# GpSimd makes the sign words of a float64-to-float32 weight conversion, and VectorE folds the shift into the or

## The chip, the cores and the metric

The kernel runs on one core of one Trainium2 chip. The metric is device time in microseconds for one execution. A core has five engines that work side by side, each in its own program order: TensorE (PE, matrix products, with its weight loads shown as PEld), VectorE (DVE), ScalarE (ACT), GpSimd (POOL) and SyncE (SP, which here issues the transfers). An engine waits for another only through semaphores.

## The reference

What is computed is linear attention with a root-mean-square norm, and on its output a feed-forward layer whose activation is a rational function:

```python
kv = np.einsum('bhsd,bhse->bhde', k, v)          # q, k, v: (8, 8, 576, 64) float32
out = np.einsum('bhsd,bhde->bhse', q, kv)
rms = np.sqrt(np.mean(out * out, axis=-1, keepdims=True) + 1e-06)
attn = (out / rms * g_norm).astype(np.float32)
...
h = x @ w_in                                     # x: (4608, 512), w_in: (512, 2048)
P = a[0] + a[1] * h + a[2] * h**2 + a[3] * h**3
Q = 1.0 + np.abs(b[0]) * np.abs(h) + np.abs(b[1]) * h**2
g = P / (Q + 1e-06)
return (g @ w_out).astype(np.float32)            # w_out: (2048, 512)
```

The weights `w_in` and `w_out` come as float64. The kernel sees them as pairs of 32-bit words and makes float32 of them on the chip.

## The kernel before, in words

**Tiles.** The 4608 tokens are nine tiles of 512, and the 2048 hidden columns are sixteen chunks of 128. A step of the main loop, here called a slot, is one pair (tile t, chunk c). There are 144, numbered i from 0; slots 0 to 15 belong to tile 0. In slot i, PE makes `h` of slot i+1 (`gemm1`, L409 for tile 0, L413 to L415 later), some of the attention of the next tile, and the share of slot i-2 in the output (`gemm2`, L470 for tile 0 and four chunks of tile 1, L474 to L476 otherwise). In tile 0 the products run in plain float32: four for `h` and four for the output in a slot, each of which the trace shows as two matrix instructions, so x8 is one slot's worth. Later tiles use split operands and three products for each.

**The activation of a slot** runs on ACT and DVE, in the order of the code:

- `ew_a`: ACT makes d = h squared (L423), q = |b0 h| (L424) and u = -a3 h - a2 (L426). DVE makes q = b1 d + q (L425) and u = u h (L427).
- `ew_b`: `fill(-1)`, then DVE u = (u - a1) h (L433). ACT makes d = 1/(1+q) with a logarithm and an exponential (L434, L435), which need L425.
- `ew_c`: DVE L439 (q and d, so it needs L435), `fill(0)`, L441, `fill(1)`, L447, `fill(2)`.

L427 and L433 read `h` in PSUM and `u` in SBUF. L425, L439, L441 and L447 read two tiles in SBUF each. The buffer of `h` is free for the next product after L433.

**The fills.** `rest[k]` lists other DVE work that is put at these four places in a slot's DVE order: the conversion of weights, the remainders of splits, parts of the attention. Every engine's order is the order of the code (a manual schedule).

**The conversion** of a unit of two chunks (128 by 1024 words) has two stages. `conv_a`: ACT scales the high and the low words (L179; for the first unit DVE, L177). `conv_b`, on DVE: L193 shifts the high word left by three, L198 takes the sign bit of the high word and ors it in, L199 adds the low word. There are 16 units, eight of `w_in` ("wi") and eight of `w_out` ("wo"). The first three are converted in halves: the first one ahead of the loop, the first half of the second too, its second half and the first half of the third in slot 0, and the last half in slot 1. The other 13 are converted whole, one in each of the slots 2 to 14, with L193 at `fill(-1)` and L198 and L199 at `fill(0)`. From tile 1 on the loop has no conversions.

What waits for a conversion: L409 of the chunks of a "wi" unit, and L470 of those of a "wo" unit. A unit of slot 3, say, holds w_out chunks 2 and 3, and PE's output product for slot 2 needs it.

Of the kernel before, what the change touches and what calls it, by code (L numbers as in the profile page):

```python
# [9 lines left out]
I32 = mybir.dt.int32  # L10
# [3 lines left out]
ALU = mybir.AluOpType  # L14
# [9 lines left out]
def linear_attention_then_rational_ffn(  # L24
# [13 lines left out]
    PE, ACT, DVE, POOL = nc.tensor, nc.scalar, nc.vector, nc.gpsimd  # L38
# [31 lines left out]
    na = const.tile([P, 4], F32, name="na")  # L70
    POOL.tensor_scalar(na, ab[:, 0:4], -1.0, None, ALU.mult)
    b1abs = const.tile([P, 1], F32, name="b1abs")
# [67 lines left out]
    units = list(schedule)  # L140
# [3 lines left out]
    def at_slot(step, k):  # L144
        return [u for u in units if schedule[u][step] == k]
# [7 lines left out]
    raws, ups, w32, whl, gparts = {}, {}, {}, {}, {}  # L153

    def fetch_w(u):
        kind, c = u
        k = units.index(u) % NG
        raws[u] = wpool.tile([P, 2 * DM], I64, tag=f"g{k}", name=f"raw_{kind}{c}")
        src = w_in[c:c + 2].rearrange("c p k f -> p c (k f)") if kind == "wi" else \
            w_out[c:c + 2].rearrange("c p f -> p c f")  # L160
        to = raws[u].rearrange("p (c f) -> p c f", c=2)
        for js in ((slice(0, 1), slice(1, 2)) if u in units[:2] else (slice(0, 2),)):
            nc.sync.dma_start(to[:, js], src[:, js])
# [5 lines left out]
    def words(u, part):  # L169
        w = raws[u].bitcast(I32).rearrange("p (f w) -> p f w", w=2)[:, part]  # L170
        return w[:, :, 0], w[:, :, 1]

    both, one, two = slice(0, 2 * DM), slice(0, DM), slice(DM, 2 * DM)
# [7 lines left out]
    def conv_a(u, part=both, engine="S"):  # L181
        low, high = words(u, part)
        scale(engine, f32(high), f32(high), 2.0**-112)
        scale(engine, low, low.bitcast(U32), 2.0**-29)

    def conv_b1(u, part=both):
        kind, c = u
        low, high = words(u, part)
        if u not in ups:
            ups[u] = wpool.tile([P, 2 * DM], F32, tag=f"f{units.index(u)}", name=f"{kind}w{c}")  # L190
            for j in range(2):
                w32[kind, c + j] = ups[u][:, j * DM:(j + 1) * DM]
        DVE.tensor_scalar(ups[u].bitcast(I32)[:, part], high, 3, None, ALU.logical_shift_left)  # L193

    def conv_b2(u, part=both):
        low, high = words(u, part)
        w = ups[u].bitcast(I32)[:, part]
        DVE.scalar_tensor_tensor(w, high, -(1 << 31), w, ALU.bitwise_and, ALU.bitwise_or)  # L198
        DVE.tensor_tensor(w, w, low, ALU.add)  # L199

    def conv_b(u, part=both):
        conv_b1(u, part)
        conv_b2(u, part)

    def gpart(k, j):
        if k not in gparts:
# [3 lines left out]
    def split_w(u):  # L210
        kind, c = u
        i = units.index(u)
        w = ups.pop(u)
        if i == NU - 1:
            last = work.tile([P, 2 * DM], F32, tag="rb", name="w_last", bufs=2)
            DVE.tensor_copy(last, w)
            w = last
        fpart = lambda k, what: wpool.tile([P, 2 * DM], F32R, tag=f"f{k}", name=f"{kind}{what}{c}")
        wh = fpart(i - 1, "h") if i == NU - 1 else gpart((i + 1) // 2, (i + 1) % 2)
        ACT.copy(wh, w)  # L220

        def rest():
            wl = gpart(0, 0) if i == 0 else fpart(i if i == NU - 1 else i - 1, "l")
            for j in range(2):
                js = slice(j * DM, (j + 1) * DM)
                whl[kind, c + j] = wh[:, js], wl[:, js]
            DVE.tensor_tensor(wl, w, f32(wh), ALU.subtract)  # L227
        return rest
# [171 lines left out]
    def gemm1(t, c):  # L400
        ph = ps_h.tile([P, TW], F32, tag="h", name=f"h_{t}_{c}")
        gemm1_part(t, c, ph, slice(0, TW))
        return ph
# [14 lines left out]
    def ew_a(t, c, ph, w=TW):  # L418
        nm = f"{t}_{c}"
        d = work.tile([P, w], F32, tag="d", name=f"d_{nm}")  # L420
        q = work.tile([P, w], F32, tag="q", name=f"q_{nm}")
        u = work.tile([P, w], F32, tag="u", name=f"u_{nm}")
        ACT.activation(d, ph, AF.Square)  # L423
        ACT.activation(q, ph, AF.Abs, scale=b0)  # L424
        DVE.scalar_tensor_tensor(q, d, b1abs, q, ALU.mult, ALU.add)  # L425
        ACT.activation(u, ph, AF.Identity, bias=na[:, 2:3], scale=na[:, 3:4])  # L426
        DVE.tensor_tensor(u, u, ph, ALU.mult)  # L427
        pend[t, c] = (d, q, u)

    def ew_b(t, c, ph, fill=lambda k: None):  # L430
        d, q, u = pend[t, c]
        fill(-1)
        DVE.scalar_tensor_tensor(u, u, na[:, 1:2], ph, ALU.add, ALU.mult)  # L433
        ACT.activation(d, q, AF.Ln, bias=bias[:, 2:3], scale=QSC)  # L434
        ACT.activation(d, d, AF.Exp, bias=bias[:, 3:4], scale=-1.0)  # L435

# [13 lines left out]
    def ew_d(t, c, w=TW):  # L450
        u = pend.pop((t, c))[2]
        if (t, c) in gs:
            return
        nm = f"{t}_{c}"
        gh = work.tile([P, w], F32R, tag="gh", name=f"gh_{nm}")
        gl = work.tile([P, w], F32R, tag="gl", name=f"gl_{nm}")
        ACT.copy(gh, u)
        DVE.tensor_tensor(gl, u, f32(gh), ALU.subtract)  # L458
        gs[t, c] = (gh, gl)

    def gemm2(t, c, subs=range(NSUB)):
        g = gs.pop((t, c))
        c = int(c)
        if c == 0:
            acc[t] = [ps_acc.tile([P, DM], F32, tag="acc", name=f"acc_{t}_{s}") for s in range(NSUB)]
        for k, s in enumerate(subs):
            ss = slice(k * P, (k + 1) * P)
            o = acc[t][s]
            if unsplit(t, c):
                PE.matmul(o, g[:, ss], w32["wo", c], start=(c == 0), stop=(c == NF - 1))  # L470
                continue
            gh, gl = g
            wh, wl = whl["wo", c]
            PE.matmul(o, gl[:, ss], wh, start=(c == 0), stop=False)  # L474
            PE.matmul(o, gh[:, ss], wl, start=False, stop=False)  # L475
            PE.matmul(o, gh[:, ss], wh, start=False, stop=(c == NF - 1))  # L476

    def evacuate(t):
        for k in range(NSUB // 2):
            ob = work.tile([P, 2, DM], F32, tag="rb", name=f"ob_{t}_{k}", bufs=2)  # L480
            for s in range(2):
                ACT.copy(ob[:, s], acc[t][2 * k + s])
            r0 = t * TW + 2 * k * P
            nc.sync.dma_start(out[r0:r0 + 2 * P].rearrange("(s p) d -> p s d", s=2), ob)
# [89 lines left out]
    for p in range(NPAIR):  # L574
# [2 lines left out]
        ps = slice(p * Q4, (p + 1) * Q4)  # L577
        PE.matmul(rb, spread[ps], r0[ps], start=True, stop=True)
        DVE.scalar_tensor_tensor(x0[:, p], x0[:, p], ghalf, rb, ALU.mult, ALU.mult)
    conv_b2(units[1], one)  # L580
    conv_a(units[1], two)
    conv_a(units[2])


    slots = [(t, c) for t in range(NTILE) for c in range(NF)]
    ph = gemm1(0, 0)
    for i, (t, c) in enumerate(slots[:-1]):
        ew_a(t, c, ph)
        if i:
            ew_d(*slots[i - 1])  # L590
        rest = {-1: [], 0: [], 1: [], 2: []}
        if i == 0:
            rest[-1].append(lambda: conv_b(units[1], two))
            rest[2].append(lambda: conv_b(units[2], one))
        if i == 1:
            rest[0].append(lambda: conv_b(units[2], two))
        for u in at_slot(2, i):
            rest[-1].append(lambda u=u: conv_b1(u))
            rest[0].append(lambda u=u: conv_b2(u))
        ew_b(t, c, ph, lambda k: [f() for f in rest[k]])  # L600
        for u in at_slot(3, i):
            rest[2].append(split_w(u))
        for u in at_slot(1, i):
            conv_a(u)
        if i >= LAG:
            gemm2(*slots[i - LAG])
            if slots[i - LAG][1] == NF - 1:
                evacuate(slots[i - LAG][0])
        if i < 4:
            ph = gemm1(0, i + 1)  # L610
        if t + 1 < NTILE:
            for step, p in (attention0 if t == 0 else attention)[c]:
                todo_dve = step(t + 1, p)
                if todo_dve:
                    rest[2 if t == 0 else fillat[step]].append(todo_dve)
            for u in at_slot(0, i):
                fetch_w(u)
        if 4 <= i < len(slots) - 2:
            ph = gemm1(*slots[i + 1])
        if c == NF - 2 and t < NTILE - 1:  # L620
            xl = [split(t + 1, p) for p in range(NPAIR)]
            for k in range(2):
                rest[k].append(xl[k])
                rest[2].append(xl[2 + k])
        ew_c(t, c, lambda k: [f() for f in rest[k]])
# [43 lines left out]
```

## Time and profile before

| what | value |
|---|---|
| runs shown | 919.54, 923.49, 924.40 us |
| their median | 923.49 us |
| the profiled execution | 924.01 us |
| its span, first to last instruction | 922.2 us |
| mean granted TensorE clock | 0.989 |
| DVE busy | 799.5 us, 1251 instructions |
| ACT busy | 687.8 us, 1163 instructions |
| POOL busy | 4.5 us, 32 instructions, all of them before the loop |

1.8 us of the profiled execution lie outside the span. Busy time counts an engine's instructions, not its waits. In a timeline row the columns are the start and the length in us, the engine, the line and operation, the tiles out<-in with their size, the number of instructions merged, and in brackets the idle time of that engine before it with what ended it. DVE instructions overlap a little: the next starts before the last has drained, so what a row costs in a chain is the distance from its start to the next start.

### The profile page before, as it was taken

To read this page: it belongs to the slowest core of one execution; us is meant where nothing else is said; L and a number is where in the kernel's file an instruction comes from. 1 tells how busy PE (TensorE), PEld (TensorE's weight loads), DVE (VectorE), ACT (ScalarE), POOL (GpSimd) and SP (SyncE) were. 2 spreads that over 40 slices of the span, in tenths; PEclk is the share of its full clock that TensorE was granted. 3 is DMA by queue.
4 is the path that set the end of the run, shared out by engine and by line. 5 is a ranking of instruction groups with operands and counts; after the bars stand their busy time and mean duration, and the time that the engine had idled before them with its cause. 6 is when DMAs were issued, how large, how long until landed. Compare 5 with 4: busy or idle time off the path is not lost.

```text
span 922.2 us, 11586 instructions
## 1 busy us (share of the span) xinstructions
PE 901.8 (98%) x4268; PEld 677.4 (73%) x4268; DVE 799.5 (87%) x1251; ACT 687.8 (75%) x1163; POOL 4.5 (0%) x32
## 2 busy tenths in 40 slices
PE   6889998999999999999999999999999999999998
PEld 4444444777768788878887888788887888788886
DVE  1798999999988899879977998789888988898887
ACT  2587876888777778777876787777777787777666
POOL 1000000000000000000000000000000000000000
PEclk6999999999999999999999999999999999999999
DMA  8645210320122122211131103220311020101001
GB/s 340 269 161 221 99 35 12 127 69 21 39 86 79 41 47 78 89 41 47 41 126 41 47 30 109 68 48 2 124 53 47 1 69 12 47 0 46 1 1 46
DMA packets 23840, 65.89 MB, mean 71 GB/s; under 512 B 2728, under 2 KB 2728, under 8 KB 23784
## 3 DMA queue, kind: packets, MB, share of 16 engines
q1 hardware_dynamic: 23328, 65.15, 21.5%
q8 instruction: 33, 0.54, 0.2%
q14 instruction: 23, 0.19, 0.1%
q10 hardware_dynamic: 456, 0.00, 0.0%
HBM read 55.58 MB, written 9.57 MB: 71 GB/s over the span
## 4 chain that ended last, share of the span: by engine, by line
PE 83%; DVE 12%; ACT 3%; issue 1%; DMA 1%; DVEq 0%; ACTq 0%
PE h L413 12%; PE h L415 12%; PE h L414 12%; PE acc L474 11%; PE acc L475 11%; PE acc L476 11%; PE acc L470 4%; PE h L409 2%; PE kvp L297 2%; DVE q L425 1%; DVE u L441 1%; DVE q L439 1%; DMA ab<-in_b_dram 1%; PE op L544 1%; DVE u L433 1%
## 5 line engine op out<-in xcount | busy, mean ns | idle before, releaser
L423 ACT ACTIVATE d<-h 128x512 f32<-128x512 f32 x143 | 85.8, 600 | 161.9 <-PE h L415 146.7
L413 PE MATMUL h<-x,parts 128*128 128x512 f32 (+1 forms) x516 | 205.7, 399 | 0.0
L415 PE MATMUL h<-x,parts 128*128 128x512 f32 (+1 forms) x516 | 200.5, 389 | 0.0
L475 PE MATMUL acc<-wol,gh 128*128 128x512 f32 x492 | 191.5, 389 | 0.7 <-DVE wol L227 0.7
L425 DVE SCALAR_TENSOR_TENSOR q<-d,b1abs,q 128x512 f32<-128x512 f32 x143 | 107.2, 750 | 84.8 <-ACT q L424 84.6
L414 PE MATMUL h<-x,wil 128*128 128x512 f32 (+1 forms) x452 | 175.5, 388 | 0.0
L474 PE MATMUL acc<-parts,gl 128*128 128x512 f32 x440 | 171.6, 390 | 0.2 <-DVE gl L458 0.2
L476 PE MATMUL acc<-parts,gh 128*128 128x512 f32 x440 | 171.2, 389 | 0.0
L434 ACT ACTIVATE d<-q,bias 128x512 f32<-128x512 f32 x143 | 105.1, 735 | 30.9 <-DVE q L425 29.4
L413 PEld LDWEIGHTS h<-x,parts 128*128 128x128 f32 x516 | 96.9, 188 | 26.4 <-DVE gl L458 5.0
L426 ACT ACTIVATE u<-h,na 128x512 f32<-128x512 f32 x143 | 112.1, 784 | 0.0
L415 PEld LDWEIGHTS h<-x,parts 128*128 128x128 f32 x516 | 96.9, 188 | 20.6
L475 PEld LDWEIGHTS acc<-wol,gh 128*128 128x128 f32 x492 | 92.4, 188 | 20.0 <-DVE wol L227 1.0
L435 ACT ACTIVATE d<-d,bias 128x512 f32<-128x512 f32 x143 | 103.6, 724 | 4.7
L441 DVE SCALAR_TENSOR_TENSOR u<-u,na,d 128x512 f32<-128x512 f32 x143 | 106.7, 746 | 0.0
L433 DVE SCALAR_TENSOR_TENSOR u<-u,na,h 128x512 f32<-128x512 f32 x143 | 106.1, 742 | 0.2
L439 DVE SCALAR_TENSOR_TENSOR q<-q,d 128x512 f32<-128x512 f32 x143 | 98.6, 689 | 1.1 <-ACT d L435 1.1
L427 DVE TENSOR_TENSOR u<-u,h 128x512 f32<-128x512 f32 x143 | 97.9, 685 | 0.9
L424 ACT ACTIVATE q<-h,ab 128x512 f32<-128x512 f32 x143 | 98.1, 686 | 0.0
L414 PEld LDWEIGHTS h<-x,wil 128*128 128x128 f32 x452 | 85.0, 188 | 16.2 <-issue 0.2
L474 PEld LDWEIGHTS acc<-parts,gl 128*128 128x128 f32 x440 | 82.6, 188 | 18.5 <-DVE gl L458 1.1
L476 PEld LDWEIGHTS acc<-parts,gh 128*128 128x128 f32 x440 | 82.6, 188 | 17.1
(137 smaller groups left out, 1087.4 us busy)
## 6 DMA issues: line engine op xcount, KB each, us to landing
kvm<-in_kv_dram SPq DMA_DIRECT2D x28, 640.0 KB
raw_wo<-in_w_out_dram SPq DMA_DIRECT2D x8, 1024.0 KB
qr<-in_qT_dram SPq DMA_DIRECT2D x32, 256.0 KB
out_dram<-ob SPq DMA_DIRECT2D x16, 512.0 KB
rb<-rd SPq DMA_DIRECT2D x28, 256.0 KB
raw_wi<-in_w_in_dram SPq DMA_DIRECT2D x6, 1024.0 KB
first<-in_first_dram SPq DMA_DIRECT2D x4, 896.0 KB
raw_wi<-in_w_in_dram SPq DMA_DIRECT2D x4, 512.0 KB
```

Of the source, the lines that this page charges most:

```text
L413: PE.matmul(ph, wh, xl, start=(kc == 0), stop=False)
L414: PE.matmul(ph, wl, xh, start=False, stop=False)
L415: PE.matmul(ph, wh, xh, start=False, stop=(kc == NPAIR - 1))
L425: DVE.scalar_tensor_tensor(q, d, b1abs, q, ALU.mult, ALU.add)
L426: ACT.activation(u, ph, AF.Identity, bias=na[:, 2:3], scale=na[:, 3:4])
L433: DVE.scalar_tensor_tensor(u, u, na[:, 1:2], ph, ALU.add, ALU.mult)
L434: ACT.activation(d, q, AF.Ln, bias=bias[:, 2:3], scale=QSC)
L439: DVE.scalar_tensor_tensor(q, q, QEPS, d, ALU.add, ALU.mult)
L441: DVE.scalar_tensor_tensor(u, u, na[:, 0:1], d, ALU.add, ALU.mult)
L474: PE.matmul(o, gl[:, ss], wh, start=(c == 0), stop=False)
L475: PE.matmul(o, gh[:, ss], wl, start=False, stop=False)
L476: PE.matmul(o, gh[:, ss], wh, start=False, stop=(c == NF - 1))
```

## The change

The sign word of a unit, 0 or the sign bit alone, is made by GpSimd from the high word (`high < 0`, times -2^31). DVE then needs two operations instead of three: shift the high word and or the sign word in (one `scalar_tensor_tensor`), and add the low word. For the 13 whole units a manual dependency holds the GpSimd operation until L425 of its slot (`q_made`) is done; those of the first three units wait only for their data. In `ew_b` the DVE operation L433 moves ahead of `fill(-1)`. In slots 2 to 14 the entry at `fill(-1)` calls `conv_b2`, which issues the or there, behind L433, and puts the add (`rest`) at `fill(0)`. So DVE's order in such a slot goes from L425, L427, L193, L433, L439, L198, L199, L441, L447 to L425, L427, L433, or, L439, add, L441, L447. For the halves in slots 0 and 1 `conv_b` issues or and add together at `fill(0)` and `fill(2)`; the second half of the second unit, which stood at `fill(-1)` of slot 0, is now at `fill(0)`.

```diff
@@ conv_b1, conv_b2, conv_b
-        DVE.tensor_scalar(ups[u].bitcast(I32)[:, part], high, 3, None, ALU.logical_shift_left)
+        return POOL.tensor_scalar(ups[u].bitcast(I32)[:, part], high, 0, -float(1 << 31), ALU.is_lt, ALU.mult)
...
-        DVE.scalar_tensor_tensor(w, high, -(1 << 31), w, ALU.bitwise_and, ALU.bitwise_or)
-        DVE.tensor_tensor(w, w, low, ALU.add)
+        DVE.scalar_tensor_tensor(w, high, 3, w, ALU.logical_shift_left, ALU.bitwise_or)
+
+        def rest():
+            DVE.tensor_tensor(w, w, low, ALU.add)
+        return rest
 
     def conv_b(u, part=both):
         conv_b1(u, part)
-        conv_b2(u, part)
+        conv_b2(u, part)()
@@ ew_a
-        DVE.scalar_tensor_tensor(q, d, b1abs, q, ALU.mult, ALU.add)
+        q_made = DVE.scalar_tensor_tensor(q, d, b1abs, q, ALU.mult, ALU.add)
...
+        return q_made
@@ ew_b
         d, q, u = pend[t, c]
+        DVE.scalar_tensor_tensor(u, u, na[:, 1:2], ph, ALU.add, ALU.mult)
         fill(-1)
-        DVE.scalar_tensor_tensor(u, u, na[:, 1:2], ph, ALU.add, ALU.mult)
@@ ahead of the loop, and the loop
-    conv_b2(units[1], one)
+    conv_b2(units[1], one)()
...
+    beside = mybir.DependencyInfo(mybir.DependencyClass.Sync, mybir.DependencyReason.DATA)
...
-        ew_a(t, c, ph)
+        q_made = ew_a(t, c, ph)
+        for u in at_slot(2, i):
+
+            tc.add_manual_dep(conv_b1(u).ins, q_made.ins.name, beside, reason="sign beside h")
...
-            rest[-1].append(lambda: conv_b(units[1], two))
+            rest[0].append(lambda: conv_b(units[1], two))
...
-            rest[-1].append(lambda u=u: conv_b1(u))
-            rest[0].append(lambda u=u: conv_b2(u))
+            rest[-1].append(lambda u=u: rest[0].append(conv_b2(u)))
```

## The prediction

> **What bounds the kernel now.** First the page: which engine is busy, and through which engines the chain that ended last runs.
>
> ```profile
> PE 901.8 (98%) x4268; PEld 677.4 (73%) x4268; DVE 799.5 (87%) x1251; ACT 687.8 (75%) x1163; POOL 4.5 (0%) x32
> ...
> PE 83%; DVE 12%; ACT 3%; issue 1%; DMA 1%; DVEq 0%; ACTq 0%
> ```
>
> PE sets the pace nearly everywhere, so DVE work that goes away is worth only what PE now waits for DVE. The waits of PE from 40 us to the tail give that, all of it:
>
> ```profile
> PE acc L470 <- DVE wow L199: 4.0, 3, 2.5
> PE h L409 <- DVE u L433: 1.7, 1, 1.7
> PE h L414 <- DVE parts L227: 1.2, 1, 1.2
> PE acc L475 <- DVE wol L227: 0.7, 1, 0.7
> PE acc L474 <- DVE gl L458: 0.2, 1, 0.2
> ```
>
> That is 7.8 us, so the largest gain is of that order. About half is the very thing the change speeds up: the output product waits for a converted w_out unit. The longest of the three costs more than its wait:
>
> ```profile
> 60.36 0.80 PE L297 MATMUL kvp<-kvm 128*64 128x64 f32 x20
> 63.64 5.25 PE L470 MATMUL acc<-wow,g 128*128 128x512 f32 x8 [2.48 <-DVE wow L199]
> ```
>
> Windows cut where the granted clock changes show why the eight products behind this gap took 5.25 us (columns: length, then busy time of PE, PEld, DVE, ACT, POOL, then PEclk):
>
> ```profile
> 39.48:42.89 3.41, 2.15 (x5) 1.06 (x6) 3.38 (x6) 1.47 (x3) 0.00 (x0) 1.00 0.01 4
> ...
> 59.96:63.37 3.41, 1.20 (x22) 0.66 (x20) 3.38 (x4) 3.37 (x8) 0.00 (x0) 1.00 0.55 159
> 63.37:66.79 3.42, 3.15 (x4) 1.51 (x5) 3.31 (x8) 1.99 (x4) 0.00 (x0) 0.50 0.31 123
> ```
>
> A stretch with PE 35% busy (1.20 of 3.41) is followed by one at clock 0.50; the stretch with 63% (2.15 of 3.41) kept 1.00. Half speed for 3.42 us loses 1.7 us. The ceiling is so 7.8 + 1.7 = 9.5 us.
>
> **A whole-unit slot, before.** Slot 3 on DVE (start, length):
>
> ```profile
> 57.98 0.75 DVE L425 SCALAR_TENSOR_TENSOR q<-d,b1abs,q 128x512 f32<-128x512 f32 x1
> 58.65 0.68 DVE L427 TENSOR_TENSOR u<-u,h 128x512 f32<-128x512 f32 x1
> 59.24 0.69 DVE L193 TENSOR_SCALAR wow<-raw_wo 128x1024 int32<-128x1024 int32 x1
> 59.84 0.74 DVE L433 SCALAR_TENSOR_TENSOR u<-u,na,h 128x512 f32<-128x512 f32 x1
> 60.50 0.69 DVE L439 SCALAR_TENSOR_TENSOR q<-q,d 128x512 f32<-128x512 f32 x1
> 61.10 1.22 DVE L198 SCALAR_TENSOR_TENSOR wow<-raw_wo,wow 128x1024 int32<-128x1024 int32 x1
> 62.36 1.23 DVE L199 CUSTOM_DVE_ANT_0 wow<-raw_wo,wow 128x2048 uint16<-128x2048 uint16 x1
> ```
>
> There is no idle time in it, and L193 costs 59.84 - 59.24 = 0.60 us. The new or has the form of L198 (one shifting operand instead of a mask), so I give it the same 1.22 us, and the add that of L199. The slot's DVE work shrinks by 0.60 us, if the sign is there in time. Counting from the start of L425: L427 at 0.67, L433 at 0.67 + 0.59 = 1.26, its successor at 1.26 + 0.66 = 1.92. This successor is now the or, so the sign must be ready at 1.92. Behind a waiting or stand L439, the add, L441, L447 and the next slot's L425 on DVE, and through the add PE's L470 or L409. Behind GpSimd's own wait for L425 stands only the next sign word, and no transfer is issued from GpSimd.
>
> **The sign on GpSimd.** The trace has no operation like it; nearest are these, and PE's first product, which waits for the `zero` of the first row:
>
> ```profile
> 0.71 0.20 POOL L78 MEMSET zero<- 128x128 f32 x1 [0.29 <-POOLq L658]
> 0.86 0.95 POOL L81 MEMSET kvf<- 128x1024 f32 x1
> ...
> 7.37 0.24 POOL L71 TENSOR_SCALAR na<-ab 128x4 f32<-128x4 f32 x1 [2.43 <-DMA ab<-in_a_dram]
> 11.94 0.23 POOL L554 TENSOR_SCALAR ghalf<-gcol 128x1 f32<-128x1 f32 x1 [4.34 <-DMA gcol<-in_g_dram]
> ```
> ```profile
> 0.97 3.78 PE L528 MATMUL idle<-zero 128*128 128x128 f32 x16 [0.97 <-POOL zero L78]
> ```
>
> Lower end: the write-only 128x1024 row, 0.95 us. Upper end: the two tensor_scalar rows differ by 0.01 us over 3 elements, 0.003 us each, and 1023 of them would be some 3.5 us; these two rows are too short to trust for a slope. By the memsets an element costs (0.95 - 0.20) / 896 = 0.84 ns, and with the 0.23 us of the smallest tensor_scalar this makes 0.23 + 0.86 = 1.09 us. A read and a compare come on top of a memset, so I take 1.2 us. The wait for L425 ends at its length, 0.75; a release across engines takes about 0.06 us (`zero` ends at 0.91, PE starts at 0.97), twice. The sign is ready at 0.75 + 0.06 + 1.2 + 0.06 = 2.07, the or waits 0.15 us, and the slot gains 0.60 - 0.15 = 0.45 us; I use 0.45 below. It gains nothing if the sign takes 1.65 us, and each us above that costs a us of DVE time per slot.
>
> The Trainium skill, GPSIMD Engine Reference, section 3.1, gives about 1.8 cycles per element as the best case of a tight loop (512 elements in 769 ns); section 4.1 calls one-input operations roughly line-rate. By the first, an estimate of 1.54 us for 1024 elements, a slot would gain only about 0.1 us and the sum below would end near 922; by the second the sign would be hidden whole. No row of this trace decides between them.
>
> **The halves.** These two views show the removed operations, and slot 1, where DVE already has the new order (no L193 in front of L439):
>
> ```profile
> L193 DVE TENSOR_SCALAR wiw<-raw_wi x10: 415/686/689, 22.1 to 129.2; 128x1024 int32<-128x1024 int32 x6, 128x512 int32<-128x512 int32 x4
> L193 DVE TENSOR_SCALAR wow<-raw_wo x9: 420/685/693, 42.6 to 145.8; 128x1024 int32<-128x1024 int32 x7, 128x512 int32<-128x512 int32 x2
> ```
> ```profile
> 44.39 0.74 DVE L425 SCALAR_TENSOR_TENSOR q<-d,b1abs,q 128x512 f32<-128x512 f32 x1
> 45.05 0.68 DVE L427 TENSOR_TENSOR u<-u,h 128x512 f32<-128x512 f32 x1
> 45.76 0.75 DVE L433 SCALAR_TENSOR_TENSOR u<-u,na,h 128x512 f32<-128x512 f32 x1
> 46.67 0.69 DVE L439 SCALAR_TENSOR_TENSOR q<-q,d 128x512 f32<-128x512 f32 x1 [0.16 <-ACT d L435]
> ```
>
> With nothing between, L439 cannot start before 46.67 - 44.39 = 2.28 us after L425: ACT's exponential is late next. In the whole-unit slots the or fills that gap. Slot 0 loses two half L193 (0.42 us each) but then waits 2.28 - 1.92 = 0.36 us for ACT: gain 0.48 us. Slot 1 loses one: 0.42 us. Their signs hang on no L425 and are made long ahead, beside DVE's wait for the first `h`. Before the loop two more halves lose 0.42 us and gain a round trip to GpSimd, by the same figures 0.23 + 0.43 + 0.12 = 0.78 us, so DVE is some 0.7 us later there in all. The cover is this idle time:
>
> ```profile
> 28.39 0.69 DVE L255 SCALAR_TENSOR_TENSOR r<-ms,r 128x512 f32<-128x512 f32 x1 [1.97 <-ACT r L252]
> ```
>
> Were it gone, those 0.7 us would come off the gain.
>
> L433's move also frees the `h` buffer earlier in slot 0 and ends PE's wait of 1.7 us there. I give it no price of its own: DVE stays the bound up to 63.64, where PE then waits in any case.
>
> **The sum.** First stretch, to the product at 63.64: slots 0 and 1 give 0.48 + 0.42, slots 2 and 3 give 0.45 each: 1.8 us. PE, with its own earlier start, then stands ready at about 59.6 (in the replay the third and fourth `h`, the two output products and the small ones between run back to back from DVE's new times) and starts at 61.8: in the stretch to 63.37 it is busy 63.37 - 61.8 = 1.6 of 3.41 us, 46%, between the 35% that lost the clock and the 63% that kept it. That is nearly open; I take it as kept: 1.7 us more. Then PE bounds the loop; DVE waits for PE's `h` by way of ACT:
>
> ```profile
> DVE q L425 <- ACT q L424: 3.3, 4, 2.0
> ```
>
> (64 to 104 us.) Savings in slots 4 to 8 lengthen that wait and nothing else. From slot 10 on DVE is the bound again; between 113 and 160 us this is its only wait:
>
> ```profile
> DVE q L439 <- ACT d L435: 0.2, 1, 0.2
> ```
>
> Here PE is close behind. In slot 12 ACT has its q at 126.89 + 0.68 = 127.57, and DVE takes L425 at 127.96:
>
> ```profile
> 126.89 0.68 ACT L424 ACTIVATE q<-h,ab 128x512 f32<-128x512 f32 x1
> ```
> ```profile
> 127.96 0.74 DVE L425 SCALAR_TENSOR_TENSOR q<-d,b1abs,q 128x512 f32<-128x512 f32 x1
> ```
>
> Savings up to there bring 0.39 less a hop of 0.04, 0.35 us. Slots 12, 13 and 14, which carry attention work too, give 0.45 each: 0.35 + 1.35 = 1.7 us. From slot 15 to 172 us DVE and ACT run a chain that shifts as a whole; behind 172 PE never waits, so what is won stays won. Sum: 1.8 + 1.7 + 1.7 = 5.2 us. The profiled execution took 924.0 us (span 922.2, 1.8 outside), 0.5 above the median of the runs shown, 923.49. Forecast 924.0 - 5.2 = **918.8 us**.
>
> **The rivals.** (1) *The half clock stays*: all as above, but the shorter gap of about 2.2 us still halves the clock: 918.8 + 1.7 = 920.5. For it: 46% is no safe distance, and the gap may lie otherwise in such a stretch in another execution. (2) *The sign is not hidden*, at 1.5 to 1.9 us: slots 2 to 14 give about nothing, the halves keep 0.9 us, the clock drops as before: 923.1, with 921.5 to 925 around it. (3) *Slower: the sign becomes DVE's bound.* At 2.8 us it is ready at 0.75 + 0.12 + 2.8 = 3.67, so the slot is 3.67 - 1.92 - 0.60 = 1.15 us longer than before. Slots 2, 3 and 9 to 14 pay it in full, 9.2 us; slots 4 to 8 have 3.3 us of waiting to pay 5.75 with, 2.4 more; less 0.9: 934.7. It turns slower over all where eight times the excess passes 0.9 us, at a sign of 1.65 + 0.11 = 1.76 us, and by 0.5% at about 2.35 us. For it: the unread slope of the two small rows, and a compare no row shows; against: the memset slope. (4) *Not beside: the sign and the readers of `h` exclude each other*, so that the sign begins only behind L433, at 1.92: ready at 3.2, 0.7 us per slot lost, eight times, less 0.9: 928.7. GpSimd ran alone before, so the trace neither shows nor excludes it. The Trainium skill, SBUF — State Buffer, section "Who interferes with whom", speaks against: a VectorE instruction with at most one SBUF input does not contend with GpSimd, one with two does; L427 and L433 have one.
>
> **How the numbers follow.** Forecast 0.34, rival 1 0.26, rival 2 0.23, rival 3 0.09, rival 4 0.05, others 0.03. The range 916.5 to 926 takes in the forecast with a sign of 1.05 us (the slots' excess of 0.15 gone: five slots of the sum, 0.75, about 918) and a deeper gain from the wait at 40 us, and rivals 1 and 2; it leaves out 3 and 4. A measurement of this kernel can tell about 0.5% from no change. Faster by more than that means below 919.4: most of the forecast's share and a little of rival 1, 0.29. Slower, above 928.6: 0.13. Between: 0.58.
>
> **What would show it.** Right: 13 GpSimd rows of 128x1024 of about 1.2 us that start some 0.8 us behind L425; L425 to the or 1.9 to 2.1 us apart; L427 and L433 still 0.68 and 0.74 us; PE's waits for the add of w_out units down from 4.0 to some 2.5 us; no 0.50 in PEclk around 63 us; DVE idle less than 1 us longer ahead of the loop. Wrong: idle time ahead of the or with GpSimd as releaser above 0.6 us, longer L427 or L433, or a new wait of PE behind 172 us.

## The result: slower, and where the time went

| | before | changed |
|---|---|---|
| median of the runs | 923.75 us | 946.38 us |
| lowest to highest | 919.54 to 924.40 | 943.93 to 947.10 |
| span of the profiled execution | 922.2 us | 942.1 us |

The ratio is 1.0249, with a 95% interval of 1.0221 to 1.0277: the change costs 22.6 us where 5.2 us of gain were forecast. One execution of the kernel before, beside a later batch, took 1126.66 us at a granted clock of 0.755; it is left out everywhere. In the changed kernel the lines have moved: the q operation L425 is L429, the two readers of `h` are L431 and L437, the or is L199, the next q operation L444, the add L202, and the sign on GpSimd L194.

First GpSimd's rows, summed by shape, from the groups of the changed kernel (busy us, mean ns of one, idle time before):

```profile
L194 POOL TENSOR_SCALAR wow<-raw_wo 128x1024 int32<-128x1024 int32 x7 | 26.2, 3738 | 39.3 <-DVE q L429 32.7 <-issue 6.6
L194 POOL TENSOR_SCALAR wiw<-raw_wi 128x1024 int32<-128x1024 int32 x6 | 22.3, 3720 | 45.6 <-DVE q L429 45.6
L194 POOL TENSOR_SCALAR wiw<-raw_wi 128x512 int32<-128x512 int32 x4 | 9.0, 2252 | 8.8 <-DVE raw_wi L177 8.7
L194 POOL TENSOR_SCALAR wow<-raw_wo 128x512 int32<-128x512 int32 x2 | 3.9, 1950 | 0.0
```

The sign words of a whole unit take 3.73 us, not 1.2. Slot 3 on DVE, in order of time, shows who pays:

```profile
58.68 0.74 DVE L429 SCALAR_TENSOR_TENSOR q<-d,b1abs,q 128x512 f32<-128x512 f32 x1
59.34 0.68 DVE L431 TENSOR_TENSOR u<-u,h 128x512 f32<-128x512 f32 x1
60.06 0.75 DVE L437 SCALAR_TENSOR_TENSOR u<-u,na,h 128x512 f32<-128x512 f32 x1
63.25 1.22 DVE L199 SCALAR_TENSOR_TENSOR wow<-raw_wo,wow 128x1024 int32<-128x1024 int32 x1 [2.44 <-POOL wow L194]
64.39 0.68 DVE L444 SCALAR_TENSOR_TENSOR q<-q,d 128x512 f32<-128x512 f32 x1
65.00 1.22 DVE L202 CUSTOM_DVE_ANT_0 wow<-raw_wo,wow 128x2048 uint16<-128x2048 uint16 x1
```

Beside it ran, on GpSimd:

```profile
59.51 3.71 POOL L194 TENSOR_SCALAR wow<-raw_wo 128x1024 int32<-128x1024 int32 x1 [5.13 <-DVE q L429]
```

The sign starts 0.83 us behind the start of L429, as forecast (0.81), and the two readers of `h` keep their lengths. DVE then stands still for 2.44 us with L444, the add and the rest of the slot queued behind the or. All its waits in slots 2 to 14 are of this kind but one of 0.2 us (49 to 176 us):

```profile
DVE wow L199 <- POOL wow L194: 17.4, 7, 2.5
DVE wiw L199 <- POOL wiw L194: 14.2, 6, 2.4
```

On PE, from 40 us to the tail, the waits for a converted w_out unit grew from 4.0 to 14.6 us; the wait of 1.7 us for L433 is gone, and one for a converted w_in unit is new:

```profile
PE acc L475 <- DVE wow L202: 14.6, 7, 3.4
PE h L413 <- DVE wiw L202: 2.0, 1, 2.0
PE h L418 <- DVE parts L231: 1.5, 1, 1.5
```

Between these two traces the whole difference lies in tile 0. From slot 0's q operation to slot 15's took 154.91 - 36.88 = 118.0 us before and 174.88 - 36.78 = 138.1 us in the changed kernel, 20.1 us more; behind that the two traces run 20 us apart to the end.

But the two are not alike ahead of the loop. PE's products there ran at half speed in the trace of before, and at full speed in that of the changed kernel and in the run of the forms below (917.98 us), whose kernel is the one before with some GpSimd work on scratch tiles ahead of the loop. The same product in the trace of before, then in the run of the forms, followed by DVE's first operation on `r` in the run of the forms and in the changed kernel:

```profile
13.99 2.08 PE L544 MATMUL op<-first,kvf 128*128 128x512 f32 x2 [0.56 <-ACT kvf L540]
13.88 1.13 PE L544 MATMUL op<-first,kvf 128*128 128x512 f32 x2 [0.56 <-ACT kvf L540]
23.96 0.69 DVE L255 SCALAR_TENSOR_TENSOR r<-ms,r 128x512 f32<-128x512 f32 x1 [0.52 <-ACT r L252]
26.69 0.68 DVE L259 SCALAR_TENSOR_TENSOR r<-ms,r 128x512 f32<-128x512 f32 x1
```

Against the run of the forms the profiled execution of the changed kernel, 943.93 us, is 26.0 us longer: 4.3 us ahead of slot 0's q operation (32.45 to 36.78 us) and 21.6 us in tile 0 (116.48 to 138.10). Of the 4.3 us, 2.7 are the signs of the halves, by the last two rows; the rest goes with a stretch from 30.32 to 33.73 us in which PE's granted clock was 0.50. In the profiled execution of before, 924.01 us, a slow start (36.88 us against 32.45) and a half-clock stretch in slot 4 (9.17 us against 7.62) hide 6.0 us of the loss.

### The profile page after: what moved, and what is told of

It is laid out like the page before. It is cut to its first block, busy times and chain, and to the rows that moved or that the text cites. A ratio compares the mean times of both kernels' runs of the same rounds, so it can differ in the third digit from the quotient of the medians.

```text
span 942.1 us, 11632 instructions
## 1 busy us (share of the span) xinstructions
PE 908.4 (96%) x4268; PEld 679.3 (72%) x4268; DVE 791.1 (84%) x1232; ACT 687.0 (73%) x1163; POOL 65.9 (7%) x51
## 3 DMA queue, kind: packets, MB, share of 16 engines
HBM read 55.58 MB, written 9.57 MB: 69 GB/s over the span
## 4 chain that ended last, share of the span: by engine, by line
PE 74%; DVE 4%; ACT 2%; issue 1%; POOLq 0%; ACTq 0%; DVEq 0%
PE h L417 12%; PE h L419 12%; PE h L418 12%; PE acc L479 11%; PE acc L480 11%; PE acc L481 11%; PE kvp L301 2%; PE acc L475 1%; PE ms L345 1%; PE op L332 1%; PE op L333 1%; PE op L331 1%; DVE q L429 1%; ACT parts L224 1%; POOLq L673 0%
## 5 line engine op out<-in xcount | busy, mean ns | idle before, releaser
L427 ACT ACTIVATE d<-h 128x512 f32<-128x512 f32 x143 | 85.8, 600 | 167.7 <-PE h L419 146.8
L429 DVE SCALAR_TENSOR_TENSOR q<-d,b1abs,q 128x512 f32<-128x512 f32 x143 | 107.1, 749 | 82.4 <-ACT q L428 82.1
L439 ACT ACTIVATE d<-q,bias 128x512 f32<-128x512 f32 x143 | 105.2, 736 | 47.7 <-DVE q L429 46.6
L430 ACT ACTIVATE u<-h,na 128x512 f32<-128x512 f32 x143 | 112.1, 784 | 0.0
L480 PEld LDWEIGHTS acc<-wol,gh 128*128 128x128 f32 x492 | 92.4, 188 | 20.1 <-DVE wol L231 1.0
L437 DVE SCALAR_TENSOR_TENSOR u<-u,na,h 128x512 f32<-128x512 f32 x143 | 106.1, 742 | 0.7
L446 DVE SCALAR_TENSOR_TENSOR u<-u,na,d 128x512 f32<-128x512 f32 x143 | 106.6, 746 | 0.0
L444 DVE SCALAR_TENSOR_TENSOR q<-q,d 128x512 f32<-128x512 f32 x143 | 98.5, 689 | 1.3 <-ACT d L440 1.3
L431 DVE TENSOR_TENSOR u<-u,h 128x512 f32<-128x512 f32 x143 | 97.9, 684 | 0.9
L479 PEld LDWEIGHTS acc<-parts,gl 128*128 128x128 f32 x440 | 82.6, 188 | 18.5 <-DVE gl L463 1.1
```

What stands on the lines that cost most here:

```text
L429: q_made = DVE.scalar_tensor_tensor(q, d, b1abs, q, ALU.mult, ALU.add)
L446: DVE.scalar_tensor_tensor(u, u, na[:, 0:1], d, ALU.add, ALU.mult)
```

## The experiments

Three readings stood against each other. **Length**: the sign takes 3.73 us, and DVE's wait at the or is the whole loss. **Place**: the new order, with the or ahead of the q operation, costs by itself. **Contention**: GpSimd and DVE side by side slow each other, whatever the sign's length. Eleven kernels were run; this table sums up those that were timed more than once, and the run of the forms. "Tile 0" is the distance from the q operation of slot 0 to that of slot 15 in the profiled execution, which leaves out what varies ahead of the loop. It does not leave out the clock: a half-clock stretch in slot 4 adds some 0.9 to 1.8 us in the rows marked with a star.

| kernel | median, us | ratio to before (95%) | tile 0, us |
|---|---|---|---|
| before, beside each batch | 921.2 to 922.6 | | 118.0* |
| before, run of the forms | 918.0 (one execution) | | 116.5 |
| changed | 946.4 | 1.0249 (1.0221 to 1.0277) | 138.1 |
| no sign word | 915.9 | 0.9945 (0.9921 to 0.9970) | 112.1 |
| a quarter of it | 917.6 | 0.9969 (0.9948 to 0.9990) | 112.3 |
| half of it | 927.1 | 1.0048 (1.0026 to 1.0069) | 118.8* |
| new order, sign on DVE | 923.0 | 1.0020 (0.9993 to 1.0048) | 117.8 |
| or behind the q operation | 942.9 | 1.0224 (1.0194 to 1.0254) | 133.5* |
| sign as soon as its data is there | 927.9 | 1.0078 (1.0045 to 1.0111) | 119.5* |
| sign behind the add before | 926.4 | 1.0049 (1.0028 to 1.0071) | 118.2* |
| another form of the sign | 917.3 | 0.9949 (0.9926 to 0.9971) | 113.9* |

**No sign word.** The or takes the high word twice, so that nothing hangs on GpSimd; the manual dependency goes with it.

```diff
-        return POOL.tensor_scalar(ups[u].bitcast(I32)[:, part], high, 0, -float(1 << 31), ALU.is_lt, ALU.mult)
...
-        DVE.scalar_tensor_tensor(w, high, 3, w, ALU.logical_shift_left, ALU.bitwise_or)
+        DVE.scalar_tensor_tensor(w, high, 3, high, ALU.logical_shift_left, ALU.bitwise_or)
...
-            tc.add_manual_dep(conv_b1(u).ins, q_made.ins.name, beside, reason="sign beside h")
+            conv_b1(u)
```

> The changed kernel without the sign word: GpSimd makes nothing, and the or takes the high word as its second operand too (same form and size), so signs of weights are left out. Theory LENGTH (GpSimd's sign word takes 3.73 us where I assumed 1.2, and all of the loss is VectorE waiting for it): the rest of the prediction's sum holds, so 917 to 920 us, and no idle time ahead of the or. Rival PLACE (the or in front of the q operation, and the new order, cost time by themselves): no faster than before, 923 us or more. If the sum itself was wrong but LENGTH right: between 920 and 923.

Measured: 915.93 us, 5.3 us below before and a little below the 917 to 920 expected. PE's waits for a converted w_out unit fall from 4.0 to 2.5 us, as forecast (this kernel's lines lie one higher up):

```profile
PE acc L474 <- DVE wow L201: 2.5, 3, 1.8
```

In slots 2 to 14 of this kernel DVE waits 6.6 us, all for PE's `h` by way of ACT; in the changed kernel it waits 31.8 us, all but 0.2 of it for the sign. That is 25.2 of the 26.0 us between 112.1 and 138.1. So the order is not the cause, nor is PE's clock, since DVE hardly waits for PE in the changed kernel, and the sum behind the forecast holds when the sign costs nothing.

**A quarter of the sign.** As above, but GpSimd makes 256 columns at the changed kernel's place, and the or waits for them.

```diff
+        return POOL.tensor_scalar(ups[u].bitcast(I32)[:, part][:, 0:256], high[:, 0:256], 0, -float(1 << 31), ALU.is_lt, ALU.mult)
```

> As the kernel without the sign word, but GpSimd makes the sign of the first quarter of the columns at the changed kernel's place (256 of 1024 words for a whole unit, 256 of 512 for a half), and the or waits for it; the other signs are left out. By 1.95 us for 512 and 3.73 us for 1024 words the length is 0.17 us plus 3.48 ns a word, so 1.06 us here, a little less than the 1.2 us I assumed. LENGTH: within 2 us of the kernel without the sign, 917 to 921. Rival CONTENTION (GpSimd beside VectorE makes both slower, whatever its length): more than 3 us above the kernel without the sign, and longer rows of the two operations that read h.

Measured: 917.62 us. This is the case that the prediction described, a sign of about 1.2 us, and it is faster than before by 0.3%. GpSimd, then DVE, in slot 3:

```profile
57.39 1.10 POOL L194 TENSOR_SCALAR wow<-raw_wo 128x256 int32<-128x256 int32 x1 [5.35 <-DVE q L429]
```
```profile
56.55 0.75 DVE L429 SCALAR_TENSOR_TENSOR q<-d,b1abs,q 128x512 f32<-128x512 f32 x1
57.22 0.69 DVE L431 TENSOR_TENSOR u<-u,h 128x512 f32<-128x512 f32 x1
57.95 0.75 DVE L437 SCALAR_TENSOR_TENSOR u<-u,na,h 128x512 f32<-128x512 f32 x1
58.61 1.22 DVE L199 SCALAR_TENSOR_TENSOR wow<-raw_wo 128x1024 int32<-128x1024 int32 x1
```

The sign is over at 58.49 and the or starts at 58.61, without a wait. The readers of `h` are as long as without GpSimd: contention at this place is excluded.

**Half of the sign**, 512 columns of a whole unit, the halves of the first units in full:

> As the run with a quarter of the sign, but GpSimd makes half of it for a whole unit (512 of 1024 words, 1.95 us; the halves of the first units in full); the or waits for it, the other signs are left out. LENGTH: the or waits 0.75 + 0.12 + 1.95 - 2.05 = 0.8 us in a slot; eight slots pay it (2, 3 and 9 to 14), some 6 us above the run without the sign: 921 to 924. If the loss is a step (any use of GpSimd beyond a bound): above 930.

Measured: 927.11 us, a miss by 3 us on the upper side. DVE now waits at the or, as long as expected less 0.2 us:

```profile
54.11 0.75 DVE L437 SCALAR_TENSOR_TENSOR u<-u,na,h 128x512 f32<-128x512 f32 x1
55.45 1.23 DVE L199 SCALAR_TENSOR_TENSOR wiw<-raw_wi 128x1024 int32<-128x1024 int32 x1 [0.59 <-POOL wiw L194]
```

In tile 0 the loss against the kernel without the sign is 118.8 - 112.1 = 6.7 us, for the 6 expected; 1.8 us of it are a half-clock stretch in slot 4 (9.38 us against 7.62), so the waits cost 4.9. The rest lies ahead of the loop, where the signs of the halves are as long as in the changed kernel: slot 0's q operation is at 39.52 us here and at 37.23 there, with PE's products at half speed in both. With 1.1, 1.97 and 3.73 us of sign, tile 0 takes 112.3, 118.8 and 138.1 us: the loss grows with the length beyond the cover, and there is no step.

**The new order alone**, the three DVE operations of before in it:

```diff
-        return POOL.tensor_scalar(ups[u].bitcast(I32)[:, part], high, 0, -float(1 << 31), ALU.is_lt, ALU.mult)
+        DVE.tensor_scalar(ups[u].bitcast(I32)[:, part], high, 3, None, ALU.logical_shift_left)
...
-        DVE.scalar_tensor_tensor(w, high, 3, w, ALU.logical_shift_left, ALU.bitwise_or)
+        DVE.scalar_tensor_tensor(w, high, -(1 << 31), w, ALU.bitwise_and, ALU.bitwise_or)
...
-        for u in at_slot(2, i):
-
-            tc.add_manual_dep(conv_b1(u).ins, q_made.ins.name, beside, reason="sign beside h")
...
-            rest[-1].append(lambda u=u: rest[0].append(conv_b2(u)))
+            rest[-1].append(lambda u=u: conv_b1(u))
+            rest[0].append(lambda u=u: conv_b2(u)())
```

> VectorE makes the sign as before (shift, and-or, add), but the order is the changed one where it can be: the second read of h stands ahead of the first fill, and the half unit of slot 0 behind the q operation. LENGTH: worth little by itself, 921 to 925 us. PLACE: a good part of the loss is here, 930 or more.

Measured: 923.02 us, no difference from before that the interval shows. Place is out as the cause of 20 us, and L433's move brings nothing by itself. Trace against trace the new order even costs a little: this one kept the clock, as the run of the forms did, and its tile 0 is longer by 117.8 - 116.5 = 1.3 us.

**The or behind the q operation.**

```diff
-            rest[-1].append(lambda u=u: rest[0].append(conv_b2(u)))
+            rest[0].append(lambda u=u: conv_b2(u)())
```

> The changed kernel with the or behind the q operation instead of ahead of it; all else, and the 3.73 us of the sign, as in the changed kernel. LENGTH: the q operation fills 0.6 us of the 2.4 us of waiting in each of 13 slots, so 6 to 8 us come back, 938 to 941. PLACE as the main cause: the time returns to 925 or less. Exclusive port: the q operation, with two SBUF inputs, waits for GpSimd and nothing comes back, 945 or more.

Measured: 942.93 us; 3.5 us come back, fewer than expected. In slot 2:

```profile
54.57 0.69 DVE L444 SCALAR_TENSOR_TENSOR q<-q,d 128x512 f32<-128x512 f32 x1
56.87 1.23 DVE L199 SCALAR_TENSOR_TENSOR wiw<-raw_wi,wiw 128x1024 int32<-128x1024 int32 x1 [1.61 <-POOL wiw L194]
```

The wait shrinks from 2.33 us in that slot to 1.61, not to nothing. The q operation runs at its usual 0.69 us although GpSimd is in the middle of its sign, which started 1.46 us earlier, at 53.11.

**The sign as soon as its data is there.** Only the manual dependency goes, so that the 3.73 us lie in the slot before.

```diff
-            tc.add_manual_dep(conv_b1(u).ins, q_made.ins.name, beside, reason="sign beside h")
+            conv_b1(u)
```

> The changed kernel without the manual dependency: GpSimd makes each sign word as soon as the high word is scaled, which is in the slot before, so its 3.73 us lie beside VectorE operations with two SBUF inputs. LENGTH alone: the sign is ready long before the or, and the time is that of the kernel without the sign, 917 to 921. Rival CONTENTION (exclusive port): operations with two SBUF inputs wait until GpSimd is done, or GpSimd takes longer; single rows grow by up to 3 us, and the time stays above 930.

Measured: 927.86 us, neither 917 to 921 nor above 930. No or waits any more in slots 2 to 14, and 18.5 us come back, but one operation grows. DVE in slot 2, and the sign beside it:

```profile
53.61 1.22 DVE L199 SCALAR_TENSOR_TENSOR wiw<-raw_wi,wiw 128x1024 int32<-128x1024 int32 x1
54.75 0.68 DVE L444 SCALAR_TENSOR_TENSOR q<-q,d 128x512 f32<-128x512 f32 x1
55.35 2.13 DVE L202 CUSTOM_DVE_ANT_0 wiw<-raw_wi,wiw 128x2048 uint16<-128x2048 uint16 x1
57.40 0.74 DVE L446 SCALAR_TENSOR_TENSOR u<-u,na,d 128x512 f32<-128x512 f32 x1
```
```profile
54.85 4.14 POOL L194 TENSOR_SCALAR wow<-raw_wo 128x1024 int32<-128x1024 int32 x1 [3.15 <-ACT raw_wo L179]
```

The add takes 2.13 us instead of 1.22; L446, with two SBUF tiles too, runs at full pace while the sign goes on to 58.99. I took this for a property of the add and moved the sign behind it.

**The sign behind the add before**, a wait on the add of the slot before in place of the one on L429:

```diff
+            last_add.append(DVE.tensor_tensor(w, w, low, ALU.add))
...
-            tc.add_manual_dep(conv_b1(u).ins, q_made.ins.name, beside, reason="sign beside h")
+            tc.add_manual_dep(conv_b1(u).ins, last_add[-1].ins.name, beside, reason="sign behind the add before")
```

> The changed kernel with one edit: the sign of a whole unit hangs on the add of the slot before instead of on L425 of its own slot, so its 3.73 us lie beside the last two operations of that slot and the first three of its own, and beside no add. From the run without the sign, an add ends about 1.8 us ahead of the next slot's first operation, and the or stands 2.05 us behind that: 3.8 us for 3.73 us and two hand-overs. LENGTH with the contention seen so far (only the add grew beside GpSimd, 1.22 to 2.1 us): the or waits 0.1 us or not at all, and the time is 1 to 3 us above the run without the sign, 916 to 919, below before. If GpSimd slows other operations with two SBUF inputs as well (exclusive port): 925 or more.

Measured: 926.36 us, so my reading of the add was wrong. Now the operation that stands second behind the add grows, from 0.69 to 1.55 us (this kernel's lines lie two further down):

```profile
56.93 0.75 DVE L448 SCALAR_TENSOR_TENSOR u<-u,na,d 128x512 f32<-128x512 f32 x1
57.71 1.55 DVE L454 SCALAR_TENSOR_TENSOR g<-q,u 128x512 f32<-128x512 f32 x1
```
```profile
57.16 4.14 POOL L196 TENSOR_SCALAR wow<-raw_wo 128x1024 int32<-128x1024 int32 x1 [3.63 <-DVE wiw L204]
```

The two kernels have this in common. When the sign starts, a DVE operation with two SBUF tiles is still running: L448 here, to 56.93 + 0.75 = 57.68, and L444 in the experiment above, to 54.75 + 0.68 = 55.43. The next such operation ends as if it had begun 0.8 to 0.9 us behind that end: here at 57.71 + 1.55 - 0.69 = 58.57, 0.89 us behind it, and above at 55.35 + 2.13 - 1.22 = 56.26, 0.83 us behind it. Over the 13 signs of each of the two kernels this is 0.79 to 0.93 us; counted from the start of the sign it is 1.0 to 1.5 us. What starts later is not held. The sign pays too: it takes 3.8 to 4.2 us there. In the loop of the changed kernel no such operation starts in that time, since the readers of `h` have one SBUF tile each.

Ahead of the loop one does. There a sign of 512 words starts while the or of the half before runs, and the add behind it takes 1.01 us instead of 0.69. DVE and GpSimd in the changed kernel:

```profile
25.03 0.69 DVE L199 SCALAR_TENSOR_TENSOR wiw<-raw_wi,wiw 128x512 int32<-128x512 int32 x1 [1.86 <-POOL wiw L194]
25.76 1.01 DVE L202 CUSTOM_DVE_ANT_0 wiw<-raw_wi,wiw 128x1024 uint16<-128x1024 uint16 x1
```
```profile
25.08 2.45 POOL L194 TENSOR_SCALAR wiw<-raw_wi 128x512 int32<-128x512 int32 x1
```

By the same reckoning, with half the words, the add is held until 25.76 + 1.01 - 0.69 = 26.08, 0.36 us behind the end of the or at 25.72.

**What makes the sign long.** Six forms on 512 words, on scratch tiles, ahead of the loop:

> The kernel before with seven more GpSimd operations ahead of the loop, on scratch tiles, beside little else: a memset of 1024, then on 512 words each: the sign as changed (every second word, int32, two operations), the same on contiguous words, one operation (is_lt) on every second word, a float32 multiply, a float32 multiply and add, a float32 copy. If the length comes from the two operations, the one-operation rows take about half of 1.95 us; if from the stride, the contiguous row is shorter; if from int32, the float32 rows are; if from GpSimd's loop for any tensor_scalar, all but the copy take 1.9 us and more.

GpSimd's rows, in the order of the list (the changed form; contiguous; one compare; one float32 multiply; multiply and add; copy):

```profile
7.49 1.97 POOL L559 TENSOR_SCALAR res<-scr 128x512 int32<-128x512 int32 x1
9.54 1.92 POOL L560 TENSOR_SCALAR res<-scr 128x512 int32<-128x512 int32 x1
11.54 1.52 POOL L561 TENSOR_SCALAR res<-scr 128x512 int32<-128x512 int32 x1
13.14 1.49 POOL L562 TENSOR_SCALAR res<-scr 128x512 f32<-128x512 f32 x1
14.72 0.62 POOL L563 TENSOR_SCALAR res<-scr 128x512 f32<-128x512 f32 x1
15.40 0.61 POOL L564 COPY res<-scr 128x512 f32<-128x512 f32 x1
```

Neither stride nor type nor the number of operations explains this: two arithmetic operations are quicker than one. A second list settles the rest (multiply and add, every second word; add and multiply, every second word; float32 compare and multiply; int32 multiply and add; multiply and multiply; int32 copy):

> As the run of the forms, 512 words each, with: multiply and add on every second word in float32, add and multiply on every second word, compare and multiply on every second word in float32, multiply and add on every second word in int32, multiply and multiply on contiguous float32, an int32 copy of every second word. What is quick (0.6 us) and what is not (1.5 to 2 us) tells whether the pair of operations, the type or the stride decides; I expect the pair (multiply, add) and the copy to be quick in any type and stride.

```profile
7.74 0.65 POOL L559 TENSOR_SCALAR res<-scr 128x512 f32<-128x512 f32 x1
8.48 0.64 POOL L560 TENSOR_SCALAR res<-scr 128x512 f32<-128x512 f32 x1
9.20 1.95 POOL L561 TENSOR_SCALAR res<-scr 128x512 f32<-128x512 f32 x1
11.23 0.65 POOL L562 TENSOR_SCALAR res<-scr 128x512 int32<-128x512 int32 x1
11.97 0.62 POOL L563 TENSOR_SCALAR res<-scr 128x512 f32<-128x512 f32 x1
12.65 0.65 POOL L564 COPY res<-scr 128x512 int32<-128x512 int32 x1
```

Every pair of multiply and add that was tried is at the copy's pace; a single operation takes about 2.4 times as long, and a compare and multiply three times.

**Another form of the sign.** The sign word is the bit pattern of plus or minus zero. Multiplying the high word, read as float32, by 2^-100 underflows to it, and adding -0.0 keeps it.

```diff
-        return POOL.tensor_scalar(ups[u].bitcast(I32)[:, part], high, 0, -float(1 << 31), ALU.is_lt, ALU.mult)
+        return POOL.tensor_scalar(ups[u][:, part], f32(high), 2.0**-100, -0.0, ALU.mult, ALU.add)
```

> The changed kernel with another form of the sign word: GpSimd takes the high word as float32, multiplies it by 2^-100 and adds -0.0, so that it underflows to plus or minus zero, whose bits are the sign word; everything else as in the changed kernel. The float32 multiply and add took 0.62 us for 512 contiguous words where the compare and multiply took 1.92. If that pair keeps its pace on every second word: about 1.1 to 1.2 us for 1024, no wait at the or above 0.2 us, and the time of the run with a quarter of the sign, 915 to 919, faster than before. If the stride or the underflow throws it back to the slow pace: 3 us and more, 935 or more.

Measured: 917.32 us, ratio 0.9949 with an interval of 0.9926 to 0.9971. This version beats both kernels, before by 0.5%. GpSimd in slot 4, and DVE up to the or:

```profile
61.09 1.14 POOL L194 TENSOR_SCALAR wiw<-raw_wi 128x1024 f32<-128x1024 f32 x1 [5.64 <-DVE q L429]
```
```profile
60.26 0.75 DVE L429 SCALAR_TENSOR_TENSOR q<-d,b1abs,q 128x512 f32<-128x512 f32 x1
61.04 0.69 DVE L431 TENSOR_TENSOR u<-u,h 128x512 f32<-128x512 f32 x1
61.77 0.75 DVE L437 SCALAR_TENSOR_TENSOR u<-u,na,h 128x512 f32<-128x512 f32 x1
62.43 1.22 DVE L199 SCALAR_TENSOR_TENSOR wiw<-raw_wi,wiw 128x1024 int32<-128x1024 int32 x1
```

The same with add ahead of multiply:

> The same with the two operations exchanged: add 0.0, then multiply by 2^-100. If GpSimd is quick only for multiply then add, the sign takes 3 to 4 us and the time is 940 or more; if for any two float32 operations, 915 to 920.

One execution took 917.95 us, with 1.15 us for a sign: the order of the pair does not matter.

## Why the prediction was wrong

**The step that failed is the length of the sign**: the term of 1.2 us, made of a memset's slope and the remark that "a read and a compare come on top of a memset". It measured 3.73 us. The text weighed two estimates and took the wrong one. It had one that came out near: "the two tensor_scalar rows differ by 0.01 us over 3 elements, 0.003 us each, and 1023 of them would be some 3.5 us; these two rows are too short to trust for a slope." Those two rows were of GpSimd's tensor_scalar, though in a one-operation form, and the memset rows that I preferred were not. That their slope came so near is luck: a difference of 0.01 us is the last digit of the view, and a single multiply on 512 words took 1.49 us, 2.5 ns for each further word, where the sign took 3.5 ns. But 2.5 ns too would have put the sign at 2.8 us, beyond its cover. The operation's kind was nearer than its size.

**The form of the reckoning held.** Rival 3, the sign as DVE's bound, gives with 3.73 us: ready at 0.87 + 3.73 = 4.60, 2.08 us longer per slot; eight slots 16.6 us, five slots 10.4 less 3.3 of waiting, less 0.9 for the halves: 22.8 us, 946.8 us. The median was 946.4, but so close an agreement is luck. Between the two traces the eight slots pay 15.6 us, not 16.6, and the five slots 5.5, not 7.1; and the reckoning has nothing of the 4.3 us ahead of the loop, nor of the slow start and the half-clock stretch in the trace of before. The mechanism was right, and the chance of 0.09 too low for it.

Point by point:

- *A slot loses 0.60 us of DVE work*: right. Without the sign slots 2 and 3 take 6.45 and 6.79 us where they took 7.03 and 7.39.
- *The halves gain 0.48 and 0.42 us*: slots 0 and 1 went from 7.51 to 6.95 and from 6.56 to 6.09, 0.56 and 0.47.
- *The sum, 5.2 us*: measured without a sign 5.3, with a quarter 3.6, with the quick form 5.3 us, medians against before in its batch. Without a sign, and so without the 0.15 us of waiting in a slot, the terms were 2.1 us in slots 0 to 3, 2.15 in slots 9 to 14 and 1.7 for the clock; between the traces they were 2.2, 2.1 and 1.55.
- *The clock is kept around 63 us*: open by nature. The profiled kernels without a sign and with a quarter have no half-clock stretch in the loop, the one with the quick form has one, and so had before; but the run of the forms has none, with the loop of before, so the 1.7 us are not the change's own. In the kernel with the quick form PE was 49% busy ahead of that stretch (1.67 of 3.41 us, 55.58 to 58.99), more than the 46% that I took as enough. In the changed kernel it is worse, five such stretches in the loop, one of them twice as long, with PEclk 0.87 in the mean from 120 to 160 us.
- *Rival 2*, a sign of 1.5 to 1.9 us giving about 923: the half sign, with 1.97 us, gave 927.1, of which 2.3 us lie ahead of the loop and 1.8 us are a half-clock stretch.
- *Rival 4*, the readers of `h` and GpSimd exclude each other: wrong. Their lengths are 0.68 and 0.75 us in the changed kernel, 0.68 and 0.74 before.
- *The early halves are covered*: wrong. Each sign took 1.95 to 2.45 us, not 0.23 + 0.43, and DVE waited twice for 1.86 us. The idle time that was to cover it, 1.97 us, was that of a start at half speed; in the run of the forms it is 0.52 us. Slot 0's q operation stood at 36.78 us where it stands at 32.45 in that run; that it stood at 36.88 in the trace of before is chance.

The Trainium skill, GPSIMD Engine Reference, gives about 1.8 cycles per element as the best case of a tight loop (section 3.1), an estimate of 1.54 us for the sign, and roughly line rate for one-input operations (section 4.1). For a compare and multiply both are too short by more than half against 3.73 us; for multiply and add the run agrees with the second: 1.14 us for 1024 words, beside 1.22 us for DVE's or on as many. The measurement decides: the rate goes with the pair of operations.

## What to carry to other kernels

A long row of another operation is no price for an operation that moves to another engine, and two rows of a few words of its own kind give a warning, not a price. Where such rows disagree by a factor of three, the decision hangs on it, and one small kernel with the operation on scratch tiles settles it. Look for the form of a computation that the engine is quick at: here the same bits cost 3.73 or 1.14 us. And a wait placed in front of queued work costs its full length in every slot in which that engine is the bound, so the excess over the cover, times the number of such slots, is the price. Before two traces are compared, look whether both had the same clock: here 6 us of the reference were a slow start and one half-clock stretch.

## What the runs showed of the hardware

GpSimd's tensor_scalar has two paces: 0.62 to 0.65 us for 512 words with any pair of multiply and add that was tried, contiguous or not, float32 or int32, and 1.49 to 1.97 us with a compare or with a single operation. Which instructions run behind the two paces was not looked into.

GpSimd's hold on DVE is shorter than its instruction. Beside a sign of 1024 words, 3.8 to 4.2 us long, a DVE operation with two SBUF tiles is held until 0.8 to 0.9 us behind the end of the one that ran when the sign started, and not longer; beside 512 words until 0.36 us behind it. The Trainium skill, SBUF — State Buffer, section "Who interferes with whom", has the exclusive port, which agrees, and has it held for the whole instruction, which these rows do not bear out. That this is the time in which GpSimd reads its input is a guess, which the shorter hold with half the words fits.

PE's clock fell to half behind stretches of 3.41 us in which PE was 35% or 49% busy, and kept full pace behind one with 63%. The times of the kernel before lie in groups: near 918 us with a mean granted clock of 0.999 or 1.000, near 919.5 with 0.994, near 921.2 with 0.992, near 922.5 with 0.990, near 923.7 with 0.989, and near 924.2 with 0.997 to 0.998. Of two such executions there are traces, 917.98 us (the run of the forms) and 924.01 us: 4.4 us of their difference are the slow start, and 1.55 us the half-clock stretch in slot 4. What makes the other groups was not tried.
